# Attention gradients: some transpositions by DMA instead of TensorE

## The chip, the cores and the metric

The kernel runs on one core of a Trainium2 chip. The metric is device microseconds of that core, from launch to end, as the median of several runs. TensorE (PE) does matmuls and transpositions; PEld is its weight load; VectorE (DVE), ScalarE (ACT) and GpSimd (POOL) do elementwise work; SyncE (SP) issues the DMAs, which 16 DMA engines carry out.

## What is computed

The reference is a forward pass of four layers and its gradients. Layers 0 and 2 are linear attention blocks A with the same weights, layers 1 and 3 gated blocks B with the same weights; S = 2048 rows, D = 512, F = 1376, 32 heads of 16, bf16.

```
x = x + A(layernorm(x)); x = x + B(layernorm(x))     # twice
A: q, k, v = split(x @ wqkv);  pq, pk = phi(q), phi(k)
   kv = sum_s pk v^T;  z = sum_s pk;  o = (pq kv) / (pq z + 1e-6);  return o @ wo
B: h = sigmoid(x @ w_gate) * (x @ w_up);  return h @ w_down
outputs: x, and the gradients of x, wqkv, wo, w_gate, w_up, w_down for a given grad_out
```

## The kernel before

The 2048 rows are 16 tiles of 128. The forward pass runs the layers in order and leaves what the backward pass needs in DRAM: among it the keys `pk` as [2048, 512], the scaled queries `pqn`, `phq`, and for each attention layer the 512 x 512 products X (keys against inputs, stored at L747) and MT (L779).

The backward pass goes layer 3, 2, 1, 0. `b_bwd_p1` is a B layer; it already loads its output gradients transposed by DMA (`gT_load`, L1089, two tiles at a time from DRAM). `a_bwd_p1` (L1419) is an A layer, in two stages.

Stage 1 (L1481 to L1520), per tile `st`: four matmuls give `dp_ps` from the transposed output gradient gT and MT; ACT copies it out; `gT_make(st + 1)` transposes the next tile's gradient on PE, four blocks into `gT_ps`, and ACT copies them to `gT`; `g_cast(st + 2)` makes the bf16 copy of the gradient two tiles on; DVE does six operations; PE adds four small matmuls (`accum_dz`). After the 16 tiles come 64 matmuls for GT, and chains of small ones.

Stage 2 (L1620 to L1667), per tile: PE transposes the tile's `pk` and `dq` (L1633, four blocks each), ACT copies both into `pdT`; four matmuls give `dpk_ps`; DVE makes `dk`; `finish` of the tile before does twelve matmuls into `dh_ps` (L1606) with dqT, pkT and dkT as stationary operands; then one job of `a_small_transposes` (L1674); then dk is transposed. Tiles' `pk`, `dq`, `hT`, `h` come from DRAM in pairs, two buffers each.

`a_small_transposes` has ten jobs, one a tile: four transpose blocks of G (from GT, L1678), four of X (L1679, loaded by `load_a_weights`, L259), and one each for two small matrices `kvbd` and `dkvbd`; after the last, four stores to DRAM (L1688). At the end of the kernel `a_small_grads` (L1692) loads all of these for layers 2 and 0 and multiplies them for the gradients of wo and of a part of wqkv.

Weight gradients are a stream of their own, class `P2` (L1284): `W.run(n)` issues n units, each of 8 matmuls of 512 columns or 16 of 256; they stand between the other work of PE, and the tail of the kernel (L322 to L333) is units only, with `a_small_grads` between them. A unit's sets are prefetched two jobs ahead (L1357), a job being four units for the wide sets.

The order of instructions on PE, ACT, DVE and POOL is that of the program text (`manual_schedule`). The order of DMA issues on SP is chosen when the program is built, by when their inputs and buffers should be free; SP then takes them strictly in that order, and waits at one whose input is not ready.

Of the kernel before, what the change touches and what calls it, by code (L numbers as in the profile page):

```python
# [18 lines left out]
D = 512  # L19
# [3 lines left out]
P = 128  # L23
# [37 lines left out]
def kernel(  # L61
# [42 lines left out]
    for l in range(4):  # L104
        d = {}
        d["h"] = dram.tile([S, D], BF16, name=f"sv_h{l}")
        d["gbf"] = dram.tile([S, D], BF16, name=f"sv_gbf{l}")
        if l % 2 == 0:
            for nm in ("hT", "pqn", "phq", "pk"):
                d[nm] = dram.tile([S, D], BF16, name=f"sv_{nm}{l}")  # L110
            d["dqk"] = dram.tile([2 * D // GW, P, NST, GW], BF16, name=f"sv_dqk{l}")
            d["X"] = dram.tile([D, D], BF16, name=f"sv_X{l}")
            for nm, w in SMALL:
# [131 lines left out]
    if True:  # L245
# [4 lines left out]
        def load_a_weights(l):  # L250
            woT_GT = wb.tile([P, 2, NDC, D], BF16, name="woT_GT", tag="w_b")
            k.woT, k.GT = woT_GT[:, 0, :, :], woT_GT[:, 1, :, :]
            nc.sync.dma_start(out=k.woT, in_=k.wT["woT"].rearrange("(c p) j -> p c j", p=P))
            k.wqkvT = wb.tile([P, 3 * NDC, D], BF16, name="wqkvT", tag="w_a")
            nc.sync.dma_start(out=k.wqkvT[:], in_=k.wT["wqkvT"].rearrange("(c p) j -> p c j", p=P))
            MT_X = wb.tile([P, 2, NDC, D], BF16, name="MT_X", tag="w_c")
            k.MT, k.X_ld = MT_X[:, 0, :, :], MT_X[:, 1, :, :]
            nc.sync.dma_start(out=k.MT, in_=k.sv[l]["MT"].rearrange("(c p) j -> p c j", p=P))
            nc.sync.dma_start(out=k.X_ld, in_=k.sv[l]["X"].rearrange("(c p) j -> p c j", p=P))  # L259
        k.load_b_weights, k.load_a_weights = load_b_weights, load_a_weights  # L260

        bconst = bctx.enter_context(tc.tile_pool(name="bconst", bufs=1, reuse_waits="tile"))
# [61 lines left out]
        with tc.manual_schedule(engines=EM):  # L324
            W.run(W.left() - 58)
            W.load(0, "h", tail)
            W.run(6)
            sg = a_small_grads(k, tail, R.stage)
            next(sg)
            W.run(20)  # L330
            for _ in sg:
                W.run(3)
            W.run(W.left())  # L333
# [1085 lines left out]
def a_bwd_p1(k, R, l, W, mk_out_cb=None):  # L1419
# [6 lines left out]
    with ExitStack() as ctx:  # L1426
        ctx.enter_context(tc.manual_schedule(engines=EM))
        big = ctx.enter_context(tc.tile_pool(name=f"ab_big{l}", bufs=1, reuse_waits="tile"))
        small = ctx.enter_context(tc.tile_pool(name=f"ab_small{l}", bufs=6, reuse_waits="tile"))
        GT, X_ld = k.GT, k.X_ld  # L1430
# [5 lines left out]
        with tc.tile_pool(name=f"ab_stg1{l}", bufs=3, side="right", reuse_waits="tile") as stg, \  # L1436
# [12 lines left out]
            def g_cast(st):  # L1449
                if st < NST:  # L1450
                    nc.scalar.copy(g_all[:, st, :], k.xs[st][:])

            def gT_make(st):
                if st < NST:
                    gTs[st] = work.tile([P, NDC, P], BF16, name="gT")
                    ps = ps_tile(k, "t", [P, NDC, P], BF16, "gT_ps")
                    for c in range(NDC):
                        nc.tensor.transpose(ps[:, c, :], g_all[:, st, c * P:(c + 1) * P], k.ident[:])
                    nc.scalar.copy(gTs[st][:], ps[:])
# [27 lines left out]
            for st in range(NST):  # L1487
                ph_st = phld.get(st)
                T = dict(st=st, ph=ph_st, ph_pair=phld.cur)
                dp_ps = ps_tile(k, "g", [P, D], F32, "dp_ps")  # L1490
                gT = gTs.pop(st)
                for jc in range(NDC):
                    nc.tensor.matmul(dp_ps[:], lhsT=gT[:, jc, :], rhs=k.MT[:, jc, :],  # L1493
                                     start=(jc == 0), stop=(jc == NDC - 1))
                T["dp"] = work.tile([P, D], BF16, name="dp", bufs=6)
                nc.scalar.copy(T["dp"][:], dp_ps[:])
                gT_make(st + 1)
                g_cast(st + 2)
                prod = work.tile([P, D], BF16, name="prod", bufs=1)
                nc.vector.tensor_tensor(prod[:], T["dp"][:], pqn_all[:, st, :], ALU.mult)  # L1500
                T["cneg"] = small.tile([P, H], F32, name="cneg")
                nc.vector.tensor_reduce(T["cneg"][:], heads(prod[:]), AX.X, ALU.add, negate=True)
                T["cneg_bf"] = small.tile([P, H], BF16, name="cneg_bf", bufs=DZLAG + 3)
                nc.gpsimd.tensor_scalar(T["cneg_bf"][:], T["cneg"][:], 1.0, 0.0, ALU.mult, ALU.add)
                if st >= 1:
                    dq_ops(Ts[st - 1])
# [20 lines left out]
        with tc.tile_pool(name=f"ab_stg2{l}", bufs=2, side="right", reuse_waits="tile") as stg, \  # L1527
# [4 lines left out]
            hld = BatchLoader(k, stg, sv["h"], "h_ld", nb=NB2)  # L1532
            out_cb = mk_out_cb(stg) if mk_out_cb is not None else None
            LD, LDH = {}, {}

            def load(p):
                if p >= NST // NB2:
# [22 lines left out]
            smalls = a_small_transposes(k, l, late, GT, X_ld, dkvbdT)  # L1560

            dkv_ps = ps_tile(k, "g", [P, NDC, P], F32, "ch_ps")
            for c in range(NDC):
# [58 lines left out]
            for st in range(NST):  # L1622
# [3 lines left out]
                T = dict(st=st, h=LDH[st // NB2][:, e, :])  # L1626
                if e == 0:
                    dkst = stg.tile([P, NB2, D], BF16, name="dkstage")
                pdT = work.tile([P, 2, NDC, P], BF16, name="pdT")
                tps = ps_tile(k, "t", [P, 2, NDC, P], BF16, "T2_ps")  # L1630
                for a, src in enumerate((pk_st, dq_st)):
                    for c in range(NDC):
                        nc.tensor.transpose(tps[:, a, c, :], src[:, c * P:(c + 1) * P], k.ident[:])  # L1633
                nc.scalar.copy(pdT[:], tps[:])
                T["pdT"] = pdT
                for c in range(NDC):
                    nc.tensor.matmul(dpk_ps[:], lhsT=hT_st[:, c * P:(c + 1) * P], rhs=Nv[:, c, :],  # L1637
                                     start=False, stop=(c == NDC - 1), skip_group_check=True)
# [29 lines left out]


DZLAG = 4  # L1670
SMALL = (("G", D), ("XT", D), ("kvbd", P), ("dkvbd", P))


def a_small_transposes(k, l, pool, GT, X_ld, dkvbdT):  # L1674
    nc = k.nc
    kvbdT = k.kv[l]["kvbdT"]
    T = {nm: pool.tile([P, NDC, w], BF16, name=nm) for nm, w in SMALL}
    jobs = [(T["G"][:, c, :], [GT[:, i, c * P:(c + 1) * P] for i in range(NDC)]) for c in range(NDC)]  # L1678
    jobs += [(T["XT"][:, c, :], [X_ld[:, i, c * P:(c + 1) * P] for i in range(NDC)]) for c in range(NDC)]  # L1679
    jobs += [(T["kvbd"][:].rearrange("p c f -> p (c f)"), [kvbdT[:, c, :] for c in range(NDC)]),  # L1680
             (T["dkvbd"][:].rearrange("p c f -> p (c f)"), [dkvbdT[:, c, :] for c in range(NDC)])]
    for n, (dst, blocks) in enumerate(jobs):
        ps = ps_tile(k, "ln", [P, NDC, P], BF16, "fin_ps")
        for i, b in enumerate(blocks):
            nc.tensor.transpose(ps[:, i, :], b, k.ident[:])
        evac_copy(k, dst, ps[:].rearrange("p c f -> p (c f)"), "vector" if n % 2 else "scalar")
        yield
    for nm, w in SMALL:  # L1688
        nc.sync.dma_start(out=k.sv[l][nm].rearrange("(c p) j -> p c j", p=P), in_=T[nm][:])


def a_small_grads(k, pool, stg):  # L1692
    nc = k.nc
    T = {}
    for l in (2, 0):
        for nm, w in SMALL:
            T[nm, l] = pool.tile([P, NDC, w], BF16, name=f"{nm}_ld{l}")
            nc.sync.dma_start(out=T[nm, l][:], in_=k.sv[l][nm].rearrange("(c p) j -> p c j", p=P))
    yield
    for c in range(NDC):  # L1700
        ps = k.ps["t"].tile([P, D], F32, name="sg_ps", tag="t_ps")
        for i, l in enumerate((2, 0)):
# [5 lines left out]
    for ic in range(NDC):  # L1708
        ps = k.ps["t"].tile([P, D], F32, name="sg_ps", tag="t_ps")
        for c in range(NDC):  # L1710
            for i, l in enumerate((2, 0)):
                nc.tensor.matmul(ps[:, c * P:(c + 1) * P], lhsT=T["XT", l][:, c, ic * P:(ic + 1) * P],
                                 rhs=T["dkvbd", l][:, c, :], start=(i == 0), stop=(i == 1))
        o = stg.tile([P, D], BF16, name="fin_o")
        nc.scalar.copy(o[:], ps[:])
# [32 lines left out]
```

## Time and profile before

| | |
|---|---|
| median of 3 runs | 1188.95 us (1187.54 to 1189.41) |
| the profiled execution | 1187.47 us, of which the span of instructions is 1185.7 |
| PE | 1152.0 us busy |
| DVE, ACT, POOL | 716.4, 576.1, 289.6 us busy |
| DMA | 270.15 MB, mean 228 GB/s; queue of SP busy 73.3% of 16 engines' span |
| stage 1 and 2 of layer 2 | some 560 to 625 and 632 to 699 us |
| stage 1 and 2 of layer 0 | some 910 to 975 and 983 to 1056 us |
| tail, units and small gradients | 1054 to 1185.7 us |

Reading it: times count from the span's start. In rows of instructions "x128" is the number of them. Durations of matmuls are of the pipelined instruction, and overlap; the distance from one start to the next is what a matmul costs when PE does nothing else. "DMA share" is the mean busy share of the 16 DMA engines; packets that overlap can bring it over 1. In rows of SP the duration is that of the issue on SP's queue; the time from issue to landing is given separately.

### The profile page before, as it was taken

The page shows a single profiled execution, that of the slowest core. Times are in us where ns is not written, and L with a number is a line of the kernel's source. Part 1 is how long each engine was busy: PE and PEld are TensorE (multiplying, and loading weights), DVE is VectorE, ACT ScalarE, POOL GpSimd, SP SyncE. Part 2 cuts the span into 40 slices and gives each one's busy share as a digit, 9 for nine tenths or more (in the row PEclk, how much of TensorE's full clock was granted, in tenths as well). Part 3 has the DMA queues.
Part 4 walks back from the last instruction along what each step waited for, and adds up shares of the span by engine and source line. Part 5 has one row for each costly group of instructions (what it writes and reads, how often), then busy time and mean ns, then how long its engine had stood idle before and what let it go on. Part 6 is the DMA issues. An engine that isn't in the chain of part 4 may idle for free.

```text
span 1185.7 us, 21060 instructions
## 1 busy us (share of the span) xinstructions
PE 1152.0 (97%) x7877; PEld 698.7 (59%) x7994; DVE 716.4 (60%) x1372; ACT 576.1 (49%) x1064; POOL 289.6 (24%) x496
## 2 busy tenths in 40 slices
PE   8989999998999999999999999999999999999998
PEld 4445455444555555555546568865556755548887
DVE  6778786777777556664975750056664966751111
ACT  6667676546767734443635641143444626630010
POOL 5646665425665400000110120000000110110000
PEclk9999999999999999999999999999999999999999
DMA  8969985448445598997766979468887585749874
GB/s 265 295 194 282 283 262 177 149 164 283 144 158 182 179 274 266 308 286 238 222 199 190 288 224 344 121 172 255 263 252 256 165 289 165 231 131 334 279 201 141
DMA packets 310917, 270.15 MB, mean 228 GB/s; under 512 B 83808, under 2 KB 295712, under 8 KB 305952
## 3 DMA queue, kind: packets, MB, share of 16 engines
q1 hardware_dynamic: 310816, 268.81, 73.3%
q8 instruction: 62, 1.02, 0.4%
q14 instruction: 39, 0.32, 0.1%
HBM read 139.85 MB, written 118.85 MB: 218 GB/s over the span
## 4 chain that ended last, share of the span: by engine, by line
PE 89%; DVE 5%; DMA 2%; ACT 2%; issue 2%; POOL 0%; SPq 0%; DVEq 0%; another core or an unknown queue 0%; ACTq 0%; POOLq 0%
PE p_ps L1391 17%; PE dh_ps L1151 12%; PE dh_ps L1606 7%; PE p_ps L1375 6%; PE dhh_ps L1028 6%; PE u_ps L884 5%; PE g_ps L884 5%; PE y_ps L910 5%; PE T_ps L1111 3%; PE t_mm L600 2%; PE y_ps L848 2%; PE GT_ps L1518 2%; PE dp_ps L1493 2%; PE dpk_ps L1637 2%; PE X_ps L608 1%
## 5 line engine op out<-in xcount | busy, mean ns | idle before, releaser
L1391 PE MATMUL p_ps<-p_set,p_a 128*128 128x256 bf16 (+1 forms) x2032 | 210.3, 264 | 2.2 <-DVE dw_stg L1365 2.0
L1391 PEld LDWEIGHTS <-p_a 128*128 128x128 bf16 x2048 | 185.9, 98 | 24.3 <-issue 2.1
L1036 DVE TENSOR_TENSOR dd<-dhh_ps,ssd 128x512 bf16<-128x512 f32 x144 | 82.3, 628 | 131.7 <-PE dhh_ps L1028 126.8
L1115 ACT COPY ddT<-T_ps 128x1024 bf16<-128x1024 bf16 (+1 forms) x96 | 83.0, 867 | 133.8 <-PE T_ps L1111 133.3
L890 POOL TENSOR_TENSOR ssd_t<-hh_t,oms 128x512 bf16<-128x512 bf16 (+1 forms) x96 | 101.6, 1064 | 50.7 <-ACT out_t L226 38.3
L1151 PEld LDWEIGHTS <-ddT 128*128 128x128 bf16 (+1 forms) x704 | 68.9, 98 | 72.1
L1002 POOL TENSOR_SCALAR ab<-c 128x2 f32<-128x2 f32 x64 | 12.3, 192 | 401.0 <-DVE junk L999 385.8
L884 PEld LDWEIGHTS <-hT 128*128 128x128 bf16 x768 | 72.2, 98 | 63.2 <-DVE hT L377 1.4
L1365 DVE TENSOR_TENSOR dw_stg<-p_ps,dw_stg 128x512 bf16<-128x512 f32 (+3 forms) x43 | 28.0, 653 | 108.3 <-PE p_ps L1391 78.9
L889 DVE TENSOR_TENSOR hh_t<-u_ps,ssd_t 128x512 bf16<-128x512 f32 (+1 forms) x96 | 60.9, 634 | 53.2 <-PE u_ps L884 34.7
L884 PE MATMUL u_ps<-wu,hT 128*128 128x512 bf16 (+1 forms) x382 | 89.8, 357 | 0.1
L884 PE MATMUL g_ps<-wg,hT 128*128 128x512 bf16 (+1 forms) x354 | 84.2, 355 | 2.6 <-DVE hT L377 1.0
L1151 PE MATMUL dh_ps<-wgT,ddT 128*128 128x512 bf16 (+1 forms) x341 | 84.1, 379 | 0.4
L910 PE MATMUL y_ps<-wd,hhT 128*128 128x512 bf16 (+1 forms) x351 | 81.2, 379 | 0.7 <-DVE x L912 0.6
L1151 PE MATMUL dh_ps<-wuT,ddT 128*128 128x512 bf16 (+1 forms) x341 | 80.7, 379 | 0.6
L1375 PE MATMUL p_ps<-p_a,p_set 128*128 128x512 bf16 (+1 forms) x343 | 79.7, 379 | 0.6
L994 ACT ACTIVATE t_sb<-dh_ps,rstd_all 128x512 f32<-128x512 f32 x64 | 44.0, 687 | 72.1 <-issue 38.4
L999 DVE SCALAR_TENSOR_TENSOR junk<-t_sb,h_ld 128x512 bf16<-128x512 f32 x64 | 43.9, 686 | 49.3 <-ACT t_sb L994 48.3
L1028 PE MATMUL dhh_ps<-wdT,gTb 128*128 128x512 bf16 (+1 forms) x330 | 73.4, 357 | 0.3
L886 ACT ACTIVATE ssd_t<-g_ps 128x512 bf16<-128x512 f32 (+1 forms) x96 | 53.1, 553 | 26.8 <-PE g_ps L884 23.6
L1367 ACT CAST dw_stg<-p_ps 128x512 bf16<-128x512 f32 (+2 forms) x43 | 24.1, 560 | 64.0 <-PE p_ps L1391 57.0
L901 ACT COPY hhT<-t_tp 128x512 bf16<-128x512 bf16 (+1 forms) x96 | 49.5, 516 | 10.5 <-PE t_tp L898 10.5
(225 smaller groups left out, 2058.8 us busy)
## 6 DMA issues: line engine op xcount, KB each, us to landing
p_set<-sv_hdd SPq DMA_DIRECT2D x30, 1024.0 KB, 7.0
sv_ssd<-ssd_t SPq DMA_DIRECT2D x32, 688.0 KB, 3.7
ssd<-sv_ssd SPq DMA_DIRECT2D x24, 688.0 KB, 5.4
sv_hdd<-dd SPq DMA_DIRECT2D x48, 320.0 KB, 3.9
sv_hdd<-hh_t SPq DMA_DIRECT2D x32, 320.0 KB, 2.6
h_ld<-sv_h SPq DMA_DIRECT2D x32, 256.0 KB, 4.5
p_a<-sv_h SPq DMA_DIRECT2D x16, 512.0 KB, 6.7
p_set<-sv_dqk SPq DMA_DIRECT2D x8, 1024.0 KB, 7.1
```

The lines of the kernel that those rows point to most:

```text
L884: nc.tensor.matmul(ps[:, 0:w], lhsT=hT[:, kc, :], rhs=w_sb[:, kc, c0:c0 + w], start=(kc == 0), stop=(kc == NDC - 1))
L886: nc.scalar.activation(ssd_t[:, 0, c0:c0 + w], g_ps[:, 0:w], ACT.Sigmoid)
L889: nc.vector.tensor_tensor(hh_t[:, c0:c0 + w], u_ps[:, 0:w], ssd_t[:, 0, c0:c0 + w], ALU.mult)
L890: nc.gpsimd.tensor_tensor(ssd_t[:, 1, c0:c0 + w], hh_t[:, c0:c0 + w], oms[:, 0:w], ALU.mult)
L910: nc.tensor.matmul(y_ps[:], lhsT=T["hhT"][0:r, fc, :], rhs=k.wd[0:r, fc, :], start=(fc == 0), stop=(fc == NFC - 1))
L1028: k.nc.tensor.matmul(ps[:, 0:w], lhsT=gT[:, jc, :], rhs=k.wdT[:, jc, c0:c0 + w], start=(jc == 0), stop=(jc == NDC - 1))
L1036: k.nc.vector.tensor_tensor(dd[:, a, c0:c0 + w], ps[:, 0:w], ssd[:, a, c0:c0 + w], ALU.mult)
L1115: nc.scalar.copy(ddT[:, :, f0:f0 + nfull, :], tps[:, :, 0:nfull, :])
L1151: nc.tensor.matmul(T["dh"][:], lhsT=ddT_block(T, a, fc), rhs=(k.wuT, k.wgT)[a][0:r, fc, :], start=(i == 0), stop=(i == 2 * NFC - 1))
L1375: nc.tensor.matmul(ps[0:r, :], lhsT=set_t[:, st, c * P:c * P + r], rhs=self.ops[j["l"], "g"][:, st, :], start=(st == 0), stop=(st == NST - 1))
L1391: nc.tensor.matmul(ps[:, icl * w:(icl + 1) * w], lhsT=self.ops[j["l"], "h"][:, st, ic * P:(ic + 1) * P], rhs=set_t[:, st, 0:w], start=(st ...
L1606: nc.tensor.matmul(dh_ps[:], lhsT=lhsT, rhs=rhs, start=(i == 0), stop=(i == len(ops) - 1))
```

## The change

Four edits, in both attention layers.

Output gradients (stage 1): `gT_make` stays for tiles 0 to 7. For tiles 8 to 11 and 12 to 15 one DMA each transposes four tiles of `g_all` from SBUF to SBUF, issued in the program text at tiles 4 and 8. The casts go two a tile, so that all are made by tile 6.

Keys (stage 2): PE transposes `pk` for tiles 0 to 3 alone. For the others, DMAs of two tiles each read `pk` from DRAM transposed into `pkT`, two buffers, issued in the text at even tiles from 2 on for the next pair. `pk` itself is still loaded, for DVE.

G and X: the eight jobs a layer and the load of X go; GT is stored as it is. At the end of the kernel G and X of both layers are loaded by transposing DMAs, one after every third unit, ahead of the units that came between before (12 + 8 in place of 20).

The stores of `kvbd` and `dkvbd` follow their jobs directly.

```diff
@@ load_a_weights
-            MT_X = wb.tile([P, 2, NDC, D], BF16, name="MT_X", tag="w_c")
...
-            nc.sync.dma_start(out=k.X_ld, in_=k.sv[l]["X"].rearrange("(c p) j -> p c j", p=P))
+            k.MT = wb.tile([P, NDC, D], BF16, name="MT", tag="w_c")
+            nc.sync.dma_start(out=k.MT[:], in_=k.sv[l]["MT"].rearrange("(c p) j -> p c j", p=P))
@@ tail
             next(sg)
-            W.run(20)
+            for _ in range(2 * len(WIDE)):
+                W.run(3)
+                next(sg)
+            W.run(8)
@@ a_bwd_p1, stage 1
+            def gT_load(b):
+                t = work.tile([P, NB, NDC, P], BF16, name="gTb")
+                nc.sync.dma_start(out=t[:].rearrange("p n c t -> p (n c) t"),
+                                  in_=g_all[:, b * NB:(b + 1) * NB, :].rearrange("p n d -> p (n d)"), transpose=True)
+                for i in range(NB):
+                    gTs[b * NB + i] = t[:, i, :, :]
+
             def gT_make(st):
-                if st < NST:
+                if st < 2 * NB:
...
                 gT_make(st + 1)
-                g_cast(st + 2)
+                for c in range(2 * st + 2, 2 * st + 4):
+                    g_cast(c)
+                if st in GTLOAD:
+                    gT_load(GTLOAD[st])
@@ a_bwd_p1, stage 2
+            def load_pkT(b):
+                if b < NST // NB2:
+                    pkT[b] = stg.tile([P, NDC, NB2 * P], BF16, name="pkT")
+                    nc.sync.dma_start(out=pkT[b][:], in_=sv["pk"][batch_rows(b, NB2), :], transpose=True)
...
-                ops = [(T["pdT"][:, 1, c, :], k.wqkvT[:, c, :]) for c in range(NDC)]
-                ops += [(T["pdT"][:, 0, c, :], Mv[:, c, :]) for c in range(NDC)]
+                ops = [(T["dqT"][:, c, :], k.wqkvT[:, c, :]) for c in range(NDC)]
+                ops += [(T["pkT"][:, c, :], Mv[:, c, :]) for c in range(NDC)]
...
+                own = st < NB
...
-                for a, src in enumerate((pk_st, dq_st)):
+                for a, src in enumerate((dq_st, pk_st)[0:1 + own]):
                     for c in range(NDC):
                         nc.tensor.transpose(tps[:, a, c, :], src[:, c * P:(c + 1) * P], k.ident[:])
-                nc.scalar.copy(pdT[:], tps[:])
-                T["pdT"] = pdT
+                nc.scalar.copy(pdT[:, 0:1 + own, :, :], tps[:, 0:1 + own, :, :])
+                T["dqT"] = pdT[:, 0, :, :]
+                T["pkT"] = pdT[:, 1, :, :] if own else pkT[st // NB2][:, :, e * P:(e + 1) * P]
+                if e == 0 and st >= NB - NB2:
+                    load_pkT(st // NB2 + 1)
@@ the small transpositions
-SMALL = (("G", D), ("XT", D), ("kvbd", P), ("dkvbd", P))
+GTLOAD = {4: 2, 8: 3}
+SMALL = (("kvbd", P), ("dkvbd", P))
+WIDE = ("G", "X")
...
+    nc.sync.dma_start(out=k.sv[l]["G"].rearrange("(c p) j -> p c j", p=P), in_=GT)
+    for n, ((nm, w), src) in enumerate(zip(SMALL, (kvbdT, dkvbdT))):
+        t = pool.tile([P, NDC, w], BF16, name=nm)
         ps = ps_tile(k, "ln", [P, NDC, P], BF16, "fin_ps")
...
+        nc.sync.dma_start(out=k.sv[l][nm].rearrange("(c p) j -> p c j", p=P), in_=t[:])
         yield
@@ a_small_grads
     yield
+    for nm in WIDE:
+        for l in (2, 0):
+            T[nm, l] = t = pool.tile([P, NDC, D], BF16, name=f"{nm}T_ld{l}")
+            nc.sync.dma_start(out=t[:], in_=k.sv[l][nm][:, :], transpose=True)
+            yield
```

More of the change, by code (lines that the diff above doesn't have):

```diff
@@ L112 @@
             d["X"] = dram.tile([D, D], BF16, name=f"sv_X{l}")
+            d["G"] = dram.tile([D, D], BF16, name=f"sv_G{l}")
             for nm, w in SMALL:
@@ L255, in load_a_weights @@
             nc.sync.dma_start(out=k.wqkvT[:], in_=k.wT["wqkvT"].rearrange("(c p) j -> p c j", p=P))
-            MT_X = wb.tile([P, 2, NDC, D], BF16, name="MT_X", tag="w_c")
-            k.MT, k.X_ld = MT_X[:, 0, :, :], MT_X[:, 1, :, :]
-            nc.sync.dma_start(out=k.MT, in_=k.sv[l]["MT"].rearrange("(c p) j -> p c j", p=P))
-            nc.sync.dma_start(out=k.X_ld, in_=k.sv[l]["X"].rearrange("(c p) j -> p c j", p=P))
+            k.MT = wb.tile([P, NDC, D], BF16, name="MT", tag="w_c")
+            nc.sync.dma_start(out=k.MT[:], in_=k.sv[l]["MT"].rearrange("(c p) j -> p c j", p=P))
         k.load_b_weights, k.load_a_weights = load_b_weights, load_a_weights
@@ L1429, in a_bwd_p1 @@
         small = ctx.enter_context(tc.tile_pool(name=f"ab_small{l}", bufs=6, reuse_waits="tile"))
-        GT, X_ld = k.GT, k.X_ld
+        GT = k.GT
         dkvbdT = big.tile([P, NDC, P], BF16, name="dkvbdT")
@@ L1534, in a_bwd_p1 @@
             LD, LDH = {}, {}
+            pkT = {}
+            def load_pkT(b):
+                if b < NST // NB2:
+                    pkT[b] = stg.tile([P, NDC, NB2 * P], BF16, name="pkT")
+                    nc.sync.dma_start(out=pkT[b][:], in_=sv["pk"][batch_rows(b, NB2), :], transpose=True)
             def load(p):
@@ L1559, in a_bwd_p1 @@
             nc.gpsimd.memset(dzcpad[:], 0.0)
-            smalls = a_small_transposes(k, l, late, GT, X_ld, dkvbdT)
+            smalls = a_small_transposes(k, l, late, GT, dkvbdT)
             dkv_ps = ps_tile(k, "g", [P, NDC, P], F32, "ch_ps")
@@ L1670, with a_small_transposes @@
 DZLAG = 4
-SMALL = (("G", D), ("XT", D), ("kvbd", P), ("dkvbd", P))
-def a_small_transposes(k, l, pool, GT, X_ld, dkvbdT):
+GTLOAD = {4: 2, 8: 3}
+SMALL = (("kvbd", P), ("dkvbd", P))
+WIDE = ("G", "X")
+def a_small_transposes(k, l, pool, GT, dkvbdT):
     nc = k.nc
     kvbdT = k.kv[l]["kvbdT"]
[L1677 to L1682, printed above, removed]
+    nc.sync.dma_start(out=k.sv[l]["G"].rearrange("(c p) j -> p c j", p=P), in_=GT)
+    for n, ((nm, w), src) in enumerate(zip(SMALL, (kvbdT, dkvbdT))):
+        t = pool.tile([P, NDC, w], BF16, name=nm)
         ps = ps_tile(k, "ln", [P, NDC, P], BF16, "fin_ps")
-        for i, b in enumerate(blocks):
-            nc.tensor.transpose(ps[:, i, :], b, k.ident[:])
-        evac_copy(k, dst, ps[:].rearrange("p c f -> p (c f)"), "vector" if n % 2 else "scalar")
+        for c in range(NDC):
+            nc.tensor.transpose(ps[:, c, :], src[:, c, :], k.ident[:])
+        evac_copy(k, t[:], ps[:], "vector" if n % 2 else "scalar")
+        nc.sync.dma_start(out=k.sv[l][nm].rearrange("(c p) j -> p c j", p=P), in_=t[:])
         yield
-    for nm, w in SMALL:
-        nc.sync.dma_start(out=k.sv[l][nm].rearrange("(c p) j -> p c j", p=P), in_=T[nm][:])
 def a_small_grads(k, pool, stg):
@@ L1711, in a_small_grads @@
             for i, l in enumerate((2, 0)):
-                nc.tensor.matmul(ps[:, c * P:(c + 1) * P], lhsT=T["XT", l][:, c, ic * P:(ic + 1) * P],
+                nc.tensor.matmul(ps[:, c * P:(c + 1) * P], lhsT=T["X", l][:, c, ic * P:(ic + 1) * P],
                                  rhs=T["dkvbd", l][:, c, :], start=(i == 0), stop=(i == 1))
```

## The prediction

> **What bounds the kernel now.** I read the page from the top: the busy shares, the span in 40 slices, the chain that ended last.
>
> ```profile
> PE 1152.0 (97%) x7877; PEld 698.7 (59%) x7994; DVE 716.4 (60%) x1372; ACT 576.1 (49%) x1064; POOL 289.6 (24%) x496
> PE   8989999998999999999999999999999999999998
> PEclk9999999999999999999999999999999999999999
> DMA  8969985448445598997766979468887585749874
> PE 89%; DVE 5%; DMA 2%; ACT 2%; issue 2%; POOL 0%; SPq 0%; DVEq 0%; another core or an unknown queue 0%; ACTq 0%; POOLq 0%
> ```
>
> TensorE is busy in every slice, at full clock, and is 89% of the chain that ended last. Busy time of a pipelined engine can hide waits, so I looked next at the table by stages, for stage 1 (560 to 607 us) and stage 2 (633 to 707 us) of layer 2's attention backward, and for the stretch of the tail where G and XT are loaded. Columns: stretch, length, busy time of PE, PEld, DVE, ACT, POOL, clock, DMA share, GB/s.
>
> ```profile
> 560.00:607.00 47.00, 46.62 (x302) 23.93 (x306) 40.44 (x81) 29.72 (x55) 7.40 (x14) 1.00 0.71 220
> 633.00:707.00 74.00, 73.58 (x533) 43.32 (x540) 49.42 (x100) 45.41 (x86) 12.26 (x31) 1.00 0.78 238
> 1083.00:1113.00 30.00, 30.00 (x277) 26.89 (x275) 6.22 (x9) 0.00 (x0) 0.00 (x0) 1.00 1.03 326
> ```
>
> In all three PE has under half a microsecond free. What PE no longer does there comes off the end, unless something else becomes late. DVE, ACT and POOL are covered by PE in each; the DMA engines are full in the third.
>
> **The price of a transposition on the path.** The modelled duration of one (219 ns) overlaps its neighbours, so I take pitches, start to start, from the timeline of PE: first one tile of stage 2, then one of stage 1.
>
> ```profile
> 652.23 0.39 PE L1685 MATMUL fin_ps<-ident,woT_GT 128*128 128x128 bf16 x4
> 652.46 0.39 PE L370 MATMUL t_ps<-ident,dkstage 128*128 128x128 bf16 x4
> 652.68 0.39 PE L1633 MATMUL T_ps<-ident,pk_ld 128*128 128x128 bf16 x4
> 652.90 0.39 PE L1633 MATMUL T_ps<-ident,dq_ld 128*128 128x128 bf16 x4
> 653.13 1.03 PE L1637 MATMUL dpk_ps<-Nv,hT_ld 128*128 128x512 bf16 x4
> 594.24 0.39 PE L1458 MATMUL gT_ps<-ident,g_all 128*128 128x128 bf16 x4
> 594.47 0.24 PE L1464 MATMUL dz_ps<-cneg_bf,pqn_all 128*128 128x8 bf16 x4
> ```
>
> A group of four costs 0.225 us (652.90 less 652.68, and 594.47 less 594.24, to rounding), 56 ns each. A second reading agrees: tiles of stage 2 with a fin_ps group start 4.35 us apart (652.68, 657.03), later ones without it 4.12 (683.11, 687.23). The Trainium skill, TensorE: Matmul & The Clock Gate, Part 4: PE-mode transpose, puts one at about 275 ns in a kernel, the operand's access latency being most of it; 224 of them would then be 61.6 us. The trace does not bear that out: here they follow each other at 56 ns and the latency overlaps.
>
> **Part by part, both layers together.**
>
> 1. Output gradients, tiles 8 to 15 (L1453): 8 x 2 = 16 groups go, 16 x 0.225 = 3.6 us. The ACT copies behind them (L1459, 0.59 us each) go too; ACT was beside PE, so that is worth nothing. The casts (L1451, 0.63 us) come two a tile for the first seven tiles: ACT then has dp copy, gT copy, two casts and half an evacuation, 0.585 + 0.59 + 1.26 + 0.29 = 2.73 us, in a tile of 2.81 to 2.92 us on PE. It still fits, and the casts are ahead of their use, so I cost it at nothing; without that cover it would be below 0.2 us a tile, 14 tiles, 2.8 us.
>
> 2. Keys, tiles 4 to 15 (L1631): 12 x 2 = 24 groups, 5.4 us. The copy behind them halves (1.02 us to about 0.58), hidden.
>
> 3. The 16 small groups for G and X (L1678, L1679): 8 x 2 = 16, 3.6 us. Their copies on ACT and DVE, the load of X and the store of XT go, all beside PE. The store of G is now one of GT, of the same size.
>
> PE sheds 56 groups, 12.6 us.
>
> 4. DMA added: per layer two transposing loads of 512 KB from SBUF (gTb), six of 256 KB from DRAM (pkT), and in the tail four of 512 KB in place of four plain ones. No row shows one that reads SBUF; I take those that read DRAM, and bound it by the shortest 512 KB row and twice the longest. On the SP queue they last 1.2 to 3.8 us (gTb, 256 KB) and 1.8 to 2.9 us (wt_st, 512 KB), and land 3.0 to 9.0 and 2.9 to 6.2 us after issue.
>
> ```profile
> L1093 SPq DMA_TRANSPOSE gTb<-sv_gbf x7: 1227/1252/3768, 700.9 to 866.4; - x7
> L400 SPq DMA_TRANSPOSE wt_st<-in_A_wqkv_dram x3: 1999/2632/2880, 138.4 to 152.5; - x3
> ```
>
> In the packet records the packets of 256 B, nearly all of them transposing, last 24 ns on average, those of 1024 B 49 ns: 512 KB costs the 16 engines 2048 x 24 / 16 = 3.1 us transposed, and 512 x 49 / 16 = 1.6 us plain. The Trainium skill, Advanced Engine Details and Errata, X-Bar Transpose (TRN2), holds transposing DMAs as fast as regular ones; this trace has them near half as fast, and by the page the tail would carry no more than before.
>
> Three places have little room.
>
> (a) The first gTb load. Its casts of tiles 10 and 11 end about 576.2 us in layer 2, and its first user is the dp matmul of tile 8. If the load goes at once it lands by 576.2 + 6.2 = 582.4; if SP keeps it behind the phq_ld that it issues after a wait, by 578.9 + 6.2 = 585.1, and PE, which wants its weights 0.2 us ahead of the matmul at 584.63, waits 0.7 us. Behind the waiting PE stand only its own units. In layer 0 the same sum leaves 2 us. The second load has four tiles more.
>
> ```profile
> 578.51 0.36 SPq L1051 DMA_DIRECT2D phq_ld<-sv_phq  x1
> 584.63 1.03 PE L1493 MATMUL dp_ps<-MT_X,gT 128*128 128x512 bf16 x4
> ```
>
> (b) The loads of stage 2. In layer 2 the hT load of the last pair goes out at 685.84 and is used at 691.58; with its median of 4.3 us to landing it has 1.4 us of room. Tiles get 0.225 us shorter, so two take 0.45 of that, and a pkT issue ahead of it on SP takes 1.25. I put 0.3 us on each of the last three pairs, 0.9 us. Layer 0 issues most of these a tile earlier and has over 3 us.
>
> ```profile
> 685.84 0.41 SPq L1051 DMA_DIRECT2D hT_ld<-sv_hT  x1
> 691.58 1.03 PE L1637 MATMUL dpk_ps<-Nv,hT_ld 128*128 128x512 bf16 x3
> ```
>
> DMA share there: 0.78 x 74 = 57.7 us, plus 6 x 1.55 for pkT, less 1.6 for XT, is 65.4 us in about 69.5, 0.94.
>
> (c) The tail. A job of four units lasts 7 us and moves 1.5 MB, which at 300 GB/s is 5 us. A transposing load of 3.1 us every three units (5.25 us) asks for 0.71 + 0.59 = 1.3 of the engines for 21 us, a backlog of some 6.5 us. Sets are asked for two jobs ahead, 14 us, and land within 4.2 to 10.1 us: mostly covered. I put 1.0 us.
>
> Sum: 12.6 - 0.7 - 0.9 - 1.0 = 10.0 us. The profiled execution took 1187.47 us (span 1185.7, 1.8 around it), 1.5 under the median of 1188.95. The sum gives 1177.5 on the first and 1179.0 on the second; I say **1178**.
>
> **Rivals.**
>
> Late tiles, 1180 to 1186: the same removal, with more of it handed back. For it: the full DMA engines of the third stretch, and a load from SBUF that could take twice the 6.2 us: (a) then becomes 576.2 + 12.4 = 588.6, 4 us late in layer 2 and about 3 in layer 0; net 12.6 - 7 - 1.9 = 3.7, 1184. Against it: only the first of the two loads a layer has so little room. From about 10 us of waits on, nothing is left: the case of no change.
>
> Slower, near 1199: the pkT buffers. There are two, and the third load of a layer (pair 4) must wait until PE has finished tile 5, late in tile 6. If SP holds pk, dq and hT of the same pair behind that waiting load, hT goes out at 3.9 + 1.29 + 1.8 = 7.0 us after the start of the even tile and lands at 11.3, where it is needed at 7.8 + 0.45 = 8.25: 3.0 us late, for pairs 4 to 7 in two layers, 24.4 us, against 12.6 saved: 1187.5 + 11.8 = 1199. It decides from 1.6 us a pair on. For it: SP takes its issues strictly in order and already waits here. Against it: SP's order before shows dq and hT put behind other issues, and never ahead of a buffer that is free only a tile later, so the order would have to come out badly.
>
> Latency exposed, 1138: if each transposition held PE for its whole row of 219 ns, 224 of them would give 49 us, 1187.5 - 49. The pitches of 56 ns speak against it. By the skill's price it would be 1126. That the change doesn't do what it says can hardly be: the groups are gone from the program.
>
> **Chances and range.** Forecast (1174 to 1180) 0.60, late tiles (1180 to 1186.6) 0.20, no change 0.05, slower 0.14, latency exposed 0.01. A measurement can tell about 0.2% (2.4 us) from no change. So faster 0.81, same 0.05, slower 0.14. Range 1174 (all 12.6 us, and 0.9 for the spread of the runs) to 1186.6: 0.80; the ends of the load from SBUF lie inside.
>
> **What would show it.** Right: 224 fewer transpositions on PE; tiles of stage 2 from the fourth on 3.90 us apart without a gap; tiles 7 to 14 of stage 1 at 2.69 us instead of 2.92; no wait of PE over 1 us in either. Wrong: PE waiting for a DMA into gTb (a), hT_ld or pkT (b), or p_set (c); dq_ld and hT_ld issued behind pkT on SP; a gTb row on SP well over 3 us; DVE pacing stage 1 (six operations of a tile, L1471 to L1502, make 3.3 us already; its lag of some 0.4 us a tile is made up behind the GT matmuls that follow, 14 us).

## The result and the profile after

| | before | after |
|---|---|---|
| median of 6 runs each, taken in turn | 1188.51 us (1187.54 to 1189.41) | 1178.07 us (1173.21 to 1180.78) |
| ratio | | 0.9909, 95% interval 0.9887 to 0.9930 |
| profiled execution (span) | 1187.47 (1185.7) | 1179.22 (1177.4) |

The change takes 10.4 us off by the medians, 8.25 us between the two profiled executions. The runs after lie 7.6 us apart, those before 1.9; a cause for that spread is argued below, not shown.

The page of the kernel after, first its busy shares, its slices and its chain:

```profile
PE 1146.8 (97%) x7770; PEld 686.4 (58%) x7770; DVE 714.1 (61%) x1364; ACT 554.0 (47%) x1040; POOL 290.3 (25%) x496
PE   8989999998999999999999999999999999999898
DMA  8869984448444588996888979558896879859975
PE 85%; DVE 5%; DMA 5%; ACT 2%; issue 1%; SPq 1%; POOL 1%; DVEq 0%; POOLq 0%; ACTq 0%
```

TensorE is still busy in nearly every slice, but its share of the chain fell from 89 to 85% and that of DMA rose from 2 to 5%: the end now also follows from transfers. The table by stages, with the same three stretches (length; busy PE, PEld, DVE, ACT, POOL; clock; DMA share; GB/s):

```profile
560.00:607.00 47.00, 47.00 (x285) 23.13 (x284) 40.21 (x81) 25.66 (x48) 7.40 (x14) 1.00 0.83 245
633.00:707.00 74.00, 72.40 (x485) 41.18 (x483) 47.57 (x94) 37.90 (x81) 12.95 (x32) 1.00 0.94 253
1083.00:1113.00 30.00, 26.70 (x244) 23.46 (x243) 4.75 (x7) 0.00 (x0) 0.00 (x0) 1.00 1.11 287
```

Stage 1 is as dense as before; stage 2 of layer 2 has 1.6 us free on PE, and the tail's stretch 3.3 us. What PE waited for there, by the table of its waits (engine and line, what it waited for: us in all, times, longest):

```profile
PE p_ps L1393 <- DMA p_set<-sv_hdd: 3.2, 1, 3.2
...
PE T_ps L1652 <- DMA dq_ld<-sv_dqk: 1.1, 1, 1.1
...
PE dpk_ps L1659 <- DMA hT_ld<-sv_hT: 0.4, 1, 0.4
```

None of the three stood in the table of before. One of before's is gone, a wait of PE for VectorE's partial sums near the end, in the timeline of before:

```profile
1153.54 3.65 PE L1391 MATMUL p_ps<-p_set,p_a 128*128 128x256 bf16 x32 [1.95 <-DVE dw_stg L1365]
```

**Where the 8.25 us come from**, by the times at which the two timelines of PE pass the same instructions:

| stretch | us | what it is |
|---|---|---|
| stage 1, both layers | -1.8 and -1.6 | 16 groups of transpositions |
| stage 2 of layer 0 | -4.5 | all 20 groups, keys and G and X |
| stage 2 of layer 2 | -2.35 | the same 20 groups, less 2.1 us handed back at tile 4 |
| tail | +3.65 | the wait for p_set, 3.25, and small change |
| near the end | -1.8 | the old wait for partial sums |
| the rest | +0.2 | |

The sum is -8.2. The saving arrived, to 0.2 us, in three stages of four, and was handed back in two places. The first is tile 4 of stage 2 of layer 2. SP's timeline of the kernel after, then PE's:

```profile
629.11 0.43 SPq L1701 DMA_DIRECT2D sv_G<-woT_GT  x1
629.59 9.45 SPq L1552 DMA_TRANSPOSE pkT<-sv_pk  x2
639.22 0.45 SPq L208 DMA_DIRECT2D wgT<-wgT_d  x1
...
642.37 0.45 SPq L1053 DMA_DIRECT2D pk_ld<-sv_pk  x1
642.87 1.05 SPq L1561 DMA_DIRECT2D dq_ld<-sv_dqk  x2
644.02 0.41 SPq L1053 DMA_DIRECT2D hT_ld<-sv_hT  x1
```

```profile
646.34 0.39 PE L372 MATMUL t_ps<-ident,dkstage 128*128 128x128 bf16 x4
647.78 0.70 PE L1652 MATMUL T_ps<-ident,dq_ld 128*128 128x128 bf16 x4 [1.05 <-DMA dq_ld<-sv_dqk]
648.90 1.04 PE L1659 MATMUL dpk_ps<-Nv,hT_ld 128*128 128x512 bf16 x4 [0.42 <-DMA hT_ld<-sv_hT]
```

The brackets on PE's lines show the idle time and what ended it, 1.5 us; from start to start the two groups lost 2.1. The loads of pkT for pairs 2 and 3 stand side by side on SP and hold it for 9.45 us, and the plain loads of pair 2 go out behind them, from 642.37 on. In the kernel before the first of them went earlier:

```profile
638.77 0.81 SPq L1051 DMA_DIRECT2D pk_ld<-sv_pk  x1
```

But a second thing ends at the same time. `wgT`, weights of the next B layer, goes into the buffer in which GT lies (`woT_GT`; both have the tag `w_b`), and the kernel after stores GT from there, where the kernel before stored G from a tile of its own. That store lands 10.0 us after its issue, at 639.1, and wgT goes out at 639.22. This trace can't tell the two apart; e6_pk_late below tells more.

The second is the tail. SP's timeline there (other issues left out), and the first matmul behind the wait in PE's:

```profile
1070.67 0.33 SPq L1251 DMA_DIRECT2D p_set<-sv_hdd  x1
...
1080.74 0.45 SPq L1251 DMA_DIRECT2D p_set<-sv_hdd  x1
...
1082.27 8.66 SPq L1723 DMA_TRANSPOSE GT_ld<-sv_G  x2
...
1091.66 0.45 SPq L1251 DMA_DIRECT2D p_set<-sv_hdd  x1
...
1092.65 8.49 SPq L1723 DMA_TRANSPOSE XT_ld<-sv_X  x2
...
1101.87 0.45 SPq L1251 DMA_DIRECT2D p_set<-sv_hdd  x1
```

```profile
1109.05 7.16 PE L1393 MATMUL p_ps<-p_set,p_a 128*128 128x256 bf16 x64 [3.25 <-DMA p_set<-sv_hdd]
```

In the text the four loads stand after every third unit. On SP they stand two and two, and each two hold SP longer than a job of four units lasts (7 us). The third p_set after 1070.67 goes out at 1101.87 and PE, which wants it at 1105.8, gets it 3.25 us late.

### The profile page after: what moved, and what is told of

Read it like the earlier page. It is cut to its first block, busy times and chain, and to the rows that moved or that the text cites. A ratio compares the mean times of both kernels' runs of the same rounds, so it can differ in the third digit from the quotient of the medians.

```text
span 1177.4 us, 20705 instructions
## 1 busy us (share of the span) xinstructions
PE 1146.8 (97%) x7770; PEld 686.4 (58%) x7770; DVE 714.1 (61%) x1364; ACT 554.0 (47%) x1040; POOL 290.3 (25%) x496
## 4 chain that ended last, share of the span: by engine, by line
PE 85%; DVE 5%; DMA 5%; ACT 2%; issue 1%; SPq 1%; POOL 1%; DVEq 0%; POOLq 0%; ACTq 0%
PE p_ps L1393 15%; PE dh_ps L1153 13%; PE dh_ps L1624 7%; PE p_ps L1377 6%; PE dhh_ps L1030 6%; PE g_ps L886 5%; PE u_ps L886 5%; PE y_ps L912 4%; PE T_ps L1113 3%; PE GT_ps L1530 2%; PE dp_ps L1502 2%; PE dpk_ps L1659 2%; PE t_mm L602 2%; PE y_ps L850 2%; PE X_ps L610 2%; PE t_tp L900 1%
## 5 line engine op out<-in xcount | busy, mean ns | idle before, releaser
L886 PE MATMUL g_ps<-wg,hT 128*128 128x512 bf16 (+1 forms) x384 | 90.0, 357 | 1.0 <-DVE hT L379 1.0
L1030 PE MATMUL dhh_ps<-wdT,gTb 128*128 128x512 bf16 x336 | 74.2, 357 | 0.0
```

What stands on the lines that cost most here:

```text
L886: nc.tensor.matmul(ps[:, 0:w], lhsT=hT[:, kc, :], rhs=w_sb[:, kc, c0:c0 + w], start=(kc == 0), stop=(kc == NDC - 1))
L1030: k.nc.tensor.matmul(ps[:, 0:w], lhsT=gT[:, jc, :], rhs=k.wdT[:, jc, c0:c0 + w], start=(jc == 0), stop=(jc == NDC - 1))
```

## The experiments

Two readings of the tail were open: SP is held by the transposing loads, so that the next p_set is issued late; or their packets take time from 16 engines that are full there, and everything lands late. Each kernel ran in rounds beside the kernel before; times are medians, with the lowest and highest.

**The parts.** e1_keys_gx is the kernel after without the part of the output gradients (`if st < NST`, `g_cast(st + 2)`, no `gT_load`); e2_grads is that part alone, in the kernel before; e3_gx is the part of G and X alone. e4_free drops the 56 groups and adds no transposing load, so it leaves out the results that hang on them:

```
-  nc.sync.dma_start(out=t[:].rearrange(...), in_=g_all[...], transpose=True)    # gTb
+  gTs[b * NB + i] = g_all[:, i, :].rearrange("p (c t) -> p c t", c=NDC)
-  T["pkT"] = ... pkT[st // NB2][:, :, e * P:(e + 1) * P]
+  T["pkT"] = pdT[:, own, :, :]
-  if e == 0 and st >= NB - NB2: load_pkT(st // NB2 + 1)
-  nc.sync.dma_start(out=t[:], in_=k.sv[l][nm][:, :], transpose=True)            # G, X
+  nc.sync.dma_start(out=t[:], in_=k.sv[l][nm].rearrange("(c p) j -> p c j", p=P))
```

> The change without its part on output gradients (all 16 tiles transposed on PE, one cast a tile). Theory A (each group of four transpositions is worth its pitch of 0.225 us on PE; what is handed back comes from SP held by transposing loads while plain loads wait behind them): 16 groups more than in the changed kernel, +3.6 us, because the gradient loads made nobody wait: 1181 to 1183. Rival B (the engines' time for the transposing packets is what costs): less DMA, so less than +3.6, 1178 to 1181.

> The part on output gradients alone, in the kernel before. Theory A: 16 groups, -3.6 us against the kernel before, no wait of PE for gTb, 1184 to 1186. Rival B: -3.6 plus something for 12 us of packets, 1186 to 1189. Rival C (the gain came from the other edits, such as the load of X that went): no gain, 1188.

> The part on G and X alone. Theory A: 16 groups, -3.6 us; the wait of 2 us for a partial sum near the end of the tail may go too, and the sets that SP issues late in the tail cost some 3 us, in some executions more than in others: 1184 to 1188, with runs spread over several us. Rival B: the same time, but then with the packets, not the issue, as the cause (to be told apart by the kernel with these loads on another queue). Rival C: -2 to -5 from stores and loads that went, with no late set.

> The changed kernel without any of its new transposing loads: tiles 8 to 15 of stage 1 use untransposed gradients of tiles 0 to 3, the keys' part of stage 2 uses dq transposed in place of pk, and G and X are loaded as they are; so those results are left out. It shows what the 56 groups are worth with nothing handed back. Theory A: -12.6 us, and up to 2 more if the wait near the end goes as it did in the changed kernel: 1174 to 1176, with runs close together. Rival D (a group on the path is worth less than its pitch): 1177 to 1182.

| kernel | us | ratio, 95% interval | its price on PE alone | PE's new waits in its profile |
|---|---|---|---|---|
| before, same chip | 1187.97 (1186.95 to 1189.88) | | | |
| e2_grads | 1183.0 (1182.59 to 1185.06) | 0.9962 (0.9950 to 0.9975) | 3.6 | none |
| e3_gx | 1184.6 (1182.97 to 1186.90) | 0.9970 (0.9960 to 0.9981) | 3.6 | p_set 0.2 |
| e1_keys_gx | 1178.78 (1178.02 to 1182.61) | 0.9921 (0.9907 to 0.9935) | 9.0 | p_set 2.8 |
| e4_free | 1175.11 (1173.05 to 1175.48) | 0.9888 (0.9874 to 0.9901) | 12.6 | none |

e4_free saves 12.9 us, close to the 12.6 of 56 groups. In the profiled executions of all four the old wait for partial sums is 0.7 to 0.9 us instead of 1.95, about 1.1 us beside the price. With it, e2_grads saves 5.0 where 4.7 are to be had; its loads cost nothing. e3_gx saves 3.4 of 4.7, e1_keys_gx 9.2 of 10.1, e4_free 12.9 of 13.7, and the kernel after 10.4 of 13.7. e4_free has no new load to wait for, so this sum is good to about 0.8 us: the 3.3 us that the kernel after hands back are clear of that, the 0.9 and 1.3 of the two parts hardly.

Two of the four lie below what Theory A gave: e2_grads by 1 us, and e1_keys_gx, which came out in Rival B's range. With 16 groups more than the kernel after, 3.6 us, e1_keys_gx is only 0.7 us slower, on another chip. In its profile two pkT loads hold SP for 10.22 us at the start of stage 2, and yet PE waits for no DMA in that stage. That profile is also the slowest of its five executions (1182.61 us), so the others need not have its 2.8 us for p_set.

**Who is late: the queue or the engines?** e5_tail_act issues the four tail loads from ACT's queue; e6_pk_late puts each pkT load behind the pk, dq and hT loads of its pair on SP; e7_both does both; e8_tail_plain loads G and X in the tail plainly:

```
e5  -  nc.sync.dma_start(out=t[:], in_=k.sv[l][nm][:, :], transpose=True)
    +  nc.scalar.dma_start(out=t[:], in_=k.sv[l][nm][:, :], transpose=True)
e6  -  if e == 0 and st >= NB - NB2: load_pkT(st // NB2 + 1)
       ...
    -  load(st // NB2 + 1)
    +  last = load(st // NB2 + 1)
    +  with tc.issue_after(last.ins): load_pkT(st // NB2 + 1)
e8  +  nc.sync.dma_start(out=t[:], in_=k.sv[l][nm].rearrange("(c p) j -> p c j", p=P))
```

> The changed kernel with the four transposing loads of G and X issued from the ACT queue, idle in the tail, in place of SP; bytes and packets are the same. Theory A (SP held is the cause): no wait of PE for p_set in the tail, 3 us off, 1174 to 1176. Rival B (the engines' time): the wait stays, 1178.

> The changed kernel with each transposing load of keys ordered behind the dq, hT and pk loads of the same pair on SP. Theory A: the wait of 2.1 us of tile 4 in layer 2 goes, the rest is as before: 1175 to 1177. Rival B: the wait stays or moves to the transposed keys, 1178.

> Both of the last two: G and X from the ACT queue, keys behind the loads of their pair. Theory A: nothing is handed back, 1173 to 1175, and runs close together. Rival B: 1177 to 1179.

> The changed kernel with G and X in the tail loaded by plain DMAs from SP, so not transposed: those two gradients are wrong sums of the same work. Half the engines' time and no long hold of SP. Theory A and rival B both: the tail's wait of 3 us goes, 1174 to 1176; if it comes out as the kernel with the loads on the ACT queue, the hold is the cause, if that one stays at 1178, the packets.

| kernel | us | ratio, 95% interval | PE's waits in question |
|---|---|---|---|
| before, same chip | 1188.54 (1186.43 to 1189.73) | | |
| e5_tail_act | 1179.34 (1177.82 to 1183.76) | 0.9926 (0.9910 to 0.9942) | partial sums 4.0 in three, hT 0.2 |
| e6_pk_late | 1177.35 (1176.46 to 1178.50) | 0.9907 (0.9894 to 0.9920) | hT 1.5 in three, dq 0.6 in two, partial sums 0.2 |
| e7_both | 1179.60 (1178.13 to 1180.97) | 0.9927 (0.9915 to 0.9939) | partial sums 2.9 in three, hT 1.0 in two |
| e8_tail_plain | 1174.44 (1173.84 to 1176.22) | 0.9884 (0.9872 to 0.9897) | partial sums 0.8, hT 0.3 |

e8_tail_plain is as fast as e4_free, which ran on another chip: the loads of keys and gradients, which it keeps, cost nothing that can be measured, and the 3 us are the tail's.

e6_pk_late is a miss, and shows what the trace of the kernel after could not. No two pkT loads stand side by side any more, each holds SP for 1.2 to 2.3 us, and yet PE waits at three pairs of layer 2, 0.2 to 0.6 us at a time, 2.1 us of idle time in all against 1.5 in the kernel after. Its SP:

```profile
629.94 0.43 SPq L1705 DMA_DIRECT2D sv_G<-woT_GT  x1
640.27 0.36 SPq L208 DMA_DIRECT2D wgT<-wgT_d  x1
...
642.47 0.74 SPq L1053 DMA_DIRECT2D pk_ld<-sv_pk  x1
```

Between the first two lines SP issues nothing. It waits 9.8 us at wgT, until the store of GT has landed (10.3 us after its issue), and the loads of pair 2 go out as late as in the kernel after, 642.47 against 642.37. So the store, with wgT behind it, is enough to make them late, without any pkT load. In the kernel after and in e1 and e4 to e12, wgT goes out within 0.2 us of that landing; in e4_free the store is issued at 623.46 and wgT at 630.64, and PE does not wait in stage 2. What the pkT loads add is not shown: no kernel with both them and an early store was run.

e7_both, at 1179.60, is a miss too: PE waits 2.9 us for partial sums and 1.0 for hT. So is e5_tail_act, and a useful one. The wait for p_set is gone and the time is no better. ACT's queue and PE's waits, from its two timelines:

```profile
1045.41 1.42 ACTq L1723 DMA_TRANSPOSE GT_ld<-sv_G  x1
...
1052.26 3.61 ACTq L1723 DMA_TRANSPOSE GT_ld<-sv_G  x1
1055.98 17.13 ACTq L1723 DMA_TRANSPOSE XT_ld<-sv_X  x2
```

```profile
1072.97 14.30 PE L1393 MATMUL p_ps<-p_set,p_a 128*128 128x256 bf16 x128 [1.69 <-DVE dw_stg L1367]
1088.67 7.15 PE L1393 MATMUL p_ps<-p_set,p_a 128*128 128x256 bf16 x64 [1.40 <-DVE dw_stg L1367]
1096.77 13.48 PE L1393 MATMUL p_ps<-p_set,p_a 128*128 128x256 bf16 x122 [0.95 <-DVE dw_stg L1367]
```

ACT has nothing to wait for in the tail, so all four went out 35 to 37 us earlier than on SP, into another stretch. By the rule set down for e8_tail_plain this time speaks for the packets. But the run changed two things, the queue and the time, and so could not decide. What it does show is that such loads can cost PE time without holding SP. The first of the three waits goes back to VectorE, which by the profile waited 7.5 us for a store of weight gradients to land. SP issued that store at 1062.78, and it landed 9.3 us later (8.3 in e7_both), where the same store takes 5.4 us in e11_one_each and 5.6 in the kernel after. The DMA share from 1050 to 1075 us was 1.12, in the kernel after 0.98. The later two waits were not followed.

**One thing at a time.** e9_spread and e11_one_each leave the loads on SP and put each behind a later p_set load; in e11_one_each they come one a job, all in the full stretch, in e9_spread the first of X comes twelve units after the last of G, and the second beside the next block of the wo gradient:

```
     t = R.sets.tile(...)                                     # p_set: keep its issue
+    j["set"], self.made = p2_set(self.k, self.R, j["src"])
...
+    with tc.issue_after(W.made.ins):
         nc.sync.dma_start(out=t[:], in_=k.sv[l][nm][:, :], transpose=True)
...
-    W.run(3); next(sg)          # four times, then W.run(8)
+    W.run(4); next(sg)          # e11: four times, then W.run(4)
```

e10_plain_twice is e8_tail_plain with each load made a second time into a tile of its own (`G_more`, `X_more`), so that the engines carry as much as with the transposing loads. e12_pairs_apart is e11_one_each with the loads two and two again, 14 us between the pairs.

> The changed kernel with the four transposing loads of the tail put elsewhere on SP: each one behind a later p_set load, G of layers 2 and 0 in two different jobs, X some twenty units later, beside the blocks of the wo gradient, where the DMA share of the kernel before was 0.68. Nothing is left out. Theory A (SP is held too long by two such loads in a row, 8.5 us against a job of 7): 1174.5 to 1175.5, no p_set wait of PE over 0.5 us. Theory B (the packets of the four loads are 1.5 us each too much for engines that are full): two of four are still in the full stretch, so about half of the 3.5 us comes back, 1176 to 1177. Theory C (any transposing load in the tail costs its price wherever it stands): about 1178.

> The changed kernel with one transposing load a job, every fourth unit, each behind a later p_set load; all four stay in the full stretch, over 28 us, where the changed kernel put them two and two. Nothing is left out. Theory A (two in a row on SP): 1174.5 to 1175.5, SP held some 4.3 us four times, no p_set wait of PE over 0.5 us. Theory B (too many packets for full engines): as the changed kernel, 1177.5 to 1178.5, with a wait for p_set or for the partial sums of 2 us or more.

> The kernel with plain loads of G and X in the tail (G and X not transposed, so the gradients of wo and of v's part of wqkv are left out), and each load made twice, the second into a tile that nobody uses: 2 x 1.6 = 3.2 us of the 16 engines for each pair, as much as one transposing load. Theory A (SP held by transposing loads): as with single plain loads, 1174 to 1175, since a plain issue holds SP for little. Theory B (engines' time in a full stretch): as the changed kernel, 1177.5 to 1178.5.

> As the kernel with one transposing load a job, but two and two: both of G behind one later p_set load, both of X behind another, two jobs (14 us) apart. Nothing is left out. In the changed kernel the p_set load that PE waited for went out 11.4 us later than with one load a job (1101.87 against 1090.48), after 8.2 us of small loads, 8.7 of G and 8.5 of X with one p_set load between; from its due issue to its use lie about 15 us, of which 7 are its landing: some 8 us of room. Theory A1 (what counts is the sum of the holds that pile up ahead of one p_set): a single pair makes its p_set 5 to 6 us late, inside the room, and SP is free again before the next: 1174.5 to 1175.5, no p_set wait over 0.5 us. Theory A2 (a pair in a row is in itself too much): a p_set wait of some 3 us after each pair or after one, 1177 to 1179.

| kernel | us | before, same chip | ratio, 95% interval | PE's waits in question |
|---|---|---|---|---|
| e9_spread | 1175.12 (1174.19 to 1175.68) | 1188.46 | 0.9889 (0.9875 to 0.9903) | hT 1.2 in two, partial sums 0.9 |
| e11_one_each | 1174.76 (1173.80 to 1175.81) | 1188.46 | 0.9888 (0.9873 to 0.9902) | hT 0.8, partial sums 0.3 |
| e10_plain_twice | 1174.20 (1173.78 to 1176.56) | 1188.46 | 0.9887 (0.9871 to 0.9903) | hT 1.0 in two |
| e12_pairs_apart | 1175.55 (1174.31 to 1178.41) | 1187.28 | 0.9905 (0.9891 to 0.9919) | dq 0.7, hT 0.4 |

e10_plain_twice speaks against the engines: by the mean packet times as many engine microseconds, the DMA share of the stretch 1.09 against 1.11 in the kernel after, and no wait in the tail:

```profile
1083.00:1113.00 30.00, 30.00 (x278) 26.86 (x276) 6.22 (x9) 0.00 (x0) 0.00 (x0) 1.00 1.09 360
```

e11_one_each speaks for the queue: the same four transposing loads in the same full stretch, and no wait for p_set. Its tail on SP (other issues left out), and the table by stages:

```profile
1069.51 0.33 SPq L1251 DMA_DIRECT2D p_set<-sv_hdd  x1
...
1083.49 0.33 SPq L1251 DMA_DIRECT2D p_set<-sv_hdd  x1
...
1085.21 5.17 SPq L1723 DMA_TRANSPOSE GT_ld<-sv_G  x1
1090.48 0.53 SPq L1251 DMA_DIRECT2D p_set<-sv_hdd  x1
...
1092.18 6.00 SPq L1723 DMA_TRANSPOSE GT_ld<-sv_G  x1
1098.28 0.53 SPq L1251 DMA_DIRECT2D p_set<-sv_hdd  x1
```

```profile
1083.00:1113.00 30.00, 30.00 (x278) 26.86 (x276) 6.22 (x9) 0.00 (x0) 0.00 (x0) 1.00 1.03 268
```

A single load holds SP for 5.2 to 6.0 us, longer than the 4.3 that is the mean of two in a row; but a p_set load follows each, at most some 2 us behind its beat of 7, and PE has all its 30 us. e12_pairs_apart then shows that a pair in itself does no harm either. What decides is how much piles up on SP ahead of one p_set. Counted from the p_set load ahead of the small loads (1070.67 in the kernel after) to the third after it, in the profiled executions:

| kernel | us from that p_set to the third after it | PE's wait for p_set |
|---|---|---|
| e11_one_each, e12_pairs_apart, e9_spread | 21.0, 21.0, 21.1 | none |
| e10_plain_twice, e8_tail_plain | 22.2, 23.9 | none |
| e3_gx | 29.1 | 0.2 |
| e6_pk_late | 29.4 | none |
| the kernel after | 31.2 | 3.2 |
| e1_keys_gx | 32.1 | 2.8 |

In these profiles the two jobs of prefetch cover up to some 29 us, and above that PE waits. (Later in the tail e12_pairs_apart has one such distance of 25.2 us, 1091.33 to 1116.57, and no wait either.) In the kernel after, the p_set load that PE waits for lands 7.1 us after its issue, the median of that kernel's p_set loads from sv_hdd, so what is late is the issue. The kernels with both pairs around one p_set stand at that edge, e3_gx and e6_pk_late on one side of it, the kernel after and e1_keys_gx on the other. In the kernel after, 8.2 us of the 31.2 are the four small loads (kvbd and dkvbd, 1.5 to 2.7 us each), 17.2 the two pairs. That would also explain why its runs lie between 1173 and 1181 us: two or three microseconds more or less on SP decide. That is argued from these rows; single runs without a profile don't show it.

**A version that may be better than both.** e11_one_each leaves nothing out and takes 1174.76 us. Its interval against the kernel before overlaps that of the kernel after, and the two were not run on the same chip. But the six kernels that have nothing of the 56 groups left on PE and no pile-up in the tail (e4, e8, e9, e10, e11, e12) have medians of 1174.2 to 1175.6, and the kernel after 1178.1; e6, at 1177.4, has the pile-up without a wait for p_set, and its waits in stage 2. Of the first six, e9, e11 and e12 leave nothing out.

## Why the prediction was right, and which steps were not

**The price: right.** 56 groups at 0.225 us. In stage 1 the tiles from 8 on start 2.69 us apart, in stage 2 of layer 0 those from the fourth on 3.90, both as forecast:

```profile
584.65 1.03 PE L1502 MATMUL dp_ps<-MT,gTb 128*128 128x512 bf16 x4
587.34 1.03 PE L1502 MATMUL dp_ps<-MT,gTb 128*128 128x512 bf16 x4
590.03 1.03 PE L1502 MATMUL dp_ps<-MT,gTb 128*128 128x512 bf16 x4
...
1001.18 0.39 PE L1652 MATMUL T_ps<-ident,dq_ld 128*128 128x128 bf16 x4
1005.08 0.39 PE L1652 MATMUL T_ps<-ident,dq_ld 128*128 128x128 bf16 x4
1008.98 0.39 PE L1652 MATMUL T_ps<-ident,dq_ld 128*128 128x128 bf16 x4
```

The copies and casts cost nothing, as said: PE is busy for all 47.00 us of the stretch in stage 1. PE's weight loads fell from 7994 to 7770, by the 224 of the forecast. Latency did not show: with the 56 groups e4_free saves 12.9 us, some 1.1 of them the old wait, where the rival that gives each transposition its whole row had 49.

**(a) The first gTb load, 0.7 us: no wait.** From SBUF it lands in 4.4 to 6.0 us, and in layer 2 SP issued it at 576.98, as soon as its casts were done; there was a phq_ld ahead of it, but at 576.57 and not at 578.51, so the later of the forecast's two cases did not come. The rows of the loads that read SBUF, and of those of pkT (duration on SP in ns, shortest, median, longest):

```profile
L1457 SPq DMA_TRANSPOSE gTb<-g_all x4: 2922/2944/4005, 577.0 to 931.0; - x4
```

```profile
L1552 SPq DMA_TRANSPOSE pkT<-sv_pk x12: 1227/1406/6576, 629.6 to 1027.6; - x12
```

**(b) The loads of stage 2, 0.9 us: the wrong pair, and a term put at nothing.** The last three pairs, on which the sum puts 0.3 us each, never wait in the kernel after; pair 2 of layer 2 lost 2.1 us instead. Two steps failed. One is "a pkT issue ahead of it on SP takes 1.25": that is about the shortest, and the first two in a row took 9.45 us together. The other is "The store of G is now one of GT, of the same size", which was priced at nothing: the store now reads the buffer that wgT needs, and SP stands at wgT until it has landed. e6_pk_late shows that this alone makes the loads of pair 2 as late. Which of the two held them in the kernel after stays open, since both ended at 639.0 to 639.1. In layer 0, where the first two pkT loads hold SP for 7.23 us and no such weights follow, PE never waits. In e8 to e12, which have the same edit, the first two held SP for 7.9 to 9.4 us, and PE waited 0.3 to 1.2 us in all at pair 2 or 3 of layer 2. That the forecast's 0.9 lies in that range is luck: it stood for other pairs.

The rival of the pkT buffers came in part. From the third pkT load of a layer on, SP does wait until PE has freed the buffer, up to 3.0 us at a time in layer 0, and plain loads stand behind. But they are those of the next pair, which go out some 11 us before their use (dq of pair 5 at 1005.51, its tile at 1016.78), and nobody waits.

**(c) The tail, 1.0 us: mis-sized and mis-explained.** The step took the excess from the engines, 1.3 of them asked for over 21 us. The engines were indeed asked for more than they have (DMA share 1.11), but twice the plain packets (e10_plain_twice, 1.09) cost nothing, and one transposing load a job cost nothing. The 3.25 us came from SP: the working took the loads to go out "every three units", and SP had them two and two, behind 8.2 us of small loads. That the median was still met within 0.1 us is luck. The profiled execution handed back 5.4 us where the sum had 2.6, and a term that the sum did not have made up 1.8 of it: the old wait for partial sums was gone. Why it shrank in the variants was not isolated. And the median lies 1.15 us under that execution's time.

**The rivals.** Late tiles, no change and slower did not come. Of late tiles a part came, 5.4 us handed back in two places, but not from the loads out of SBUF, which landed in 4.4 to 6.0 us. Some of the forecast's signs of being wrong did show: PE waited for hT_ld and for p_set, dq_ld and hT_ld went out behind pkT, and one wait was over 1 us, the 1.05 for dq_ld.

## What to carry to other kernels

When PE paces a kernel, what it sheds comes off the end at the pitch of its instructions, and the transposing DMA that takes over is to be costed on the queue that issues it, not only on the engines. Look up what each issue holds its queue in the fullest stretch, add up the holds that can stand ahead of one load that PE needs, and compare the sum with the prefetch distance less the landing. Then fix the order on the queue by hand, one such load behind each load that is due: the program's order is no guide to it. Ask too which buffer a store reads: a load into that buffer waits for the store to land, with all that stands behind it on the queue (9.8 us in e6_pk_late).

## What the runs showed of the hardware

A transposing load of 512 KB in the full stretch holds its queue 5.2 to 6.0 us when alone (e11_one_each), a plain load of the same size there 0.8 to 2.9 us (e8_tail_plain); they land about equally soon, 8.0 and 8.6 us after issue in the median. A transposing load of 256 KB (pkT) holds SP 1.2 to 1.5 us from 1003 to 1030 us, where the DMA share is 0.81, and up to 6.6 in the burst at the start of stage 2 of layer 2, where it is 0.99 (629 to 639 us). Why a transposing issue holds its queue for so long in a full stretch is not shown. The Trainium skill, Advanced Engine Details and Errata, X-Bar Transpose (TRN2), holds transposing DMAs as fast as regular ones. For the landing in the tail these rows agree; of the time that an issue takes on its queue that section says nothing.

Issued early from ACT's queue, the last two took 7.9 and 9.2 us there, and the four landed up to 17.6 us after issue (e5_tail_act). Beside them a store issued from SP landed after 9.3 us, where it takes 5.4 in e11_one_each.
